# Attention and two feed-forward blocks on one core: values of the first batch on column tiles, a 16-bit sign, and a new planned order

## The chip, the cores and the metric

The program runs on one core of a Trainium2 chip. Its engines are TensorE (PE; its weight loads are listed apart as PEld), VectorE (DVE), ScalarE (ACT), GpSimd (POOL) and SyncE (SP, which here only issues DMAs). They run at the same time, each takes its own instructions in the order in which the program lists them, and semaphores tie them together. The metric is the device time of one execution in microseconds (us), lower is better.

## What is computed

```
scores = q @ k.T / 8                       # 4 batches, 8 heads, 576 x 576, head size 64
scores = where(scores >= max - tau, scores, -1e9)
x  = softmax(scores) @ v                   # 2304 x 512 when the heads stand side by side
x2 = relu(x @ w1i) ** 2 @ w1o              # 512 -> 2048 -> 512
h  = x2 @ w2i
out = (h * tanh(softplus(h))) @ w2o        # 512 -> 2048 -> 512
```

The four weight matrices come in as 64-bit floats (the kernel reads each as two 32-bit integers and builds a 32-bit float from them). Results are wanted at about the precision of 32-bit floats, so that most products are made from a high and a low part of each operand, in three matmuls instead of one.

## The kernel before

**Stages.** Tokens are cut into 9 blocks of 256. The first feed-forward block (9 token blocks, 8 slices `j` of 256 columns of the hidden layer each) can start a token block when attention has written it to DRAM; its results go to DRAM, and the second feed-forward block runs over the 9 token blocks at the end. Attention runs pair by pair (two heads side by side, 4 pairs in each of 4 batches); in a pair come units of 128 query rows (`unit`, line 703): scores on PE, a running minimum with the scaling on DVE (line 740), the exponential on ACT (line 760), the threshold with the sum on DVE (line 770), then the product with `v`.

**Two forms of attention.** Pairs of the first batch are of kind "d": their scores and values are plain 32-bit matmuls (`job_direct`, `values_direct`), and the probabilities are turned by PE transposes (line 837) and taken out of PSUM by ACT (line 850). For each of the two heads of a unit, five matmuls take a 128x128 piece of the turned probabilities as weights and 64 columns of `v` as the moving operand (line 865). Each 32-bit matmul stands in the trace as two records of weight load and matmul. The other three batches are of kind "s": a 16-bit high part (ACT, line 794) and low part (`low`, line 799, on DVE or POOL), turned by a DMA transpose.

**Weights.** Each of the four matrices is worked in 16 halves (`weights`, line 408): a load, the size by ACT (line 446), the three low bits by ACT (line 454), a clamp on DVE or POOL (line 449), the join of the two on DVE (line 461), the sign on DVE (line 467), then a high part (`to_hi`, line 495) and a low part (`to_lo`, line 505, on DVE or POOL). Layer 1's 32 halves are worked during the first 180 us, layer 2's from about 550 us on.

**Scales.** `pow2` (line 534) makes a power of two from a sum of squares, in three tiny DVE operations (lines 563, 565, 567), twice for each pair of kind "s".

**Order.** Nothing is reordered at run time. `Plan` collects every operation with its possible engines, an assumed duration on each and a due time; `order` places them by list scheduling, forwards and backwards, and so decides the order on each engine and which engine takes an operation with a choice. The numbers in `PAR` and `BIAS` shape due times and choices; buffers with a rotating choice of places (`rot`, `place`) bind the order as well. SP issues all loads and stores but the last two, in the planned order.

## Time and profile before

| | us |
|---|---|
| median of 3 runs | 1109.37 |
| lowest, highest | 1106.42, 1113.45 |
| the profiled execution | 1106.48 |
| its span, first to last instruction | 1104.7 |

The profile is of one execution. Busy time of an engine is the time in which at least one of its instructions ran; an instruction's duration holds its start-up and its tail, so durations of neighbours overlap a little. The granted clock is the share of TensorE's full clock (2.4 GHz) that it was given. Line numbers are those of the kernel before.

### The profile page before, as it was taken

The numbers are of one execution on the slowest core, as the hardware profiler recorded it, in microseconds if no ns is written. First come the engines' busy times: TensorE is split into PE (matmuls) and PEld (weight loads), VectorE is DVE, ScalarE is ACT, GpSimd is POOL, SyncE is SP. The second block draws the span as 40 slices with busy tenths as digits, with TensorE's granted clock in tenths as the row PEclk, the third lists the DMA queues.
The fourth block names the chain that finished last, engine by engine and source line by source line (L and its number), as shares of the span: only waits on it lengthen the run. The fifth ranks groups of instructions, "written<-read, shape, count | busy, mean of one in ns | idle before, by whom it ended". The sixth has DMA issues, their size and how long they took to land.

```text
span 1104.7 us, 23743 instructions
## 1 busy us (share of the span) xinstructions
PE 1071.2 (97%) x9348; PEld 967.4 (88%) x9348; DVE 743.5 (67%) x1725; ACT 775.2 (70%) x1277; POOL 84.0 (8%) x81
## 2 busy tenths in 40 slices
PE   6999989999999999999999999999999999999998
PEld 4887778888888888988999999988999889989896
DVE  4998899998797997589766149874444445443352
ACT  5788598786776876577576369977766667675584
POOL 1345021100010100010000001000000000000000
PEclk9996889999999999999999999999999999999999
DMA  8535385987777879479865024310100101000000
GB/s 239 155 108 162 94 194 125 150 175 161 154 165 144 162 155 180 78 125 167 158 206 173 25 66 146 114 59 20 39 20 20 32 9 39 20 20 20 1 20 20
DMA packets 246415, 113.75 MB, mean 103 GB/s; under 512 B 211104, under 2 KB 228000, under 8 KB 246304
## 3 DMA queue, kind: packets, MB, share of 16 engines
q1 hardware_dynamic: 246016, 111.71, 43.0%
q8 instruction: 73, 1.20, 0.4%
q10 hardware_dynamic: 288, 0.52, 0.1%
q14 instruction: 38, 0.31, 0.1%
HBM read 58.33 MB, written 14.16 MB: 66 GB/s over the span
## 4 chain that ended last, share of the span: by engine, by line
PE 74%; DVE 3%; DMA 3%; issue 1%; ACT 1%; POOL 0%; ACTq 0%; DVEq 0%; SPq 0%
PE acc L376 33%; PE h L376 19%; PE s L376 16%; PE small L376 6%; DMA pt<-hl 1%; DMA pt<-area 1%; DVE e L770 1%; DVE area L740 1%; DVE hl L799 0%; ACT e L760 0%; PE s L988 0%; ACT hl L794 0%; DVE nat L582 0%; DMA xdr<-xs 0%; DVE xo L1005 0%
## 5 line engine op out<-in xcount | busy, mean ns | idle before, releaser
L505 DVE TENSOR_TENSOR gl<-r,gh 128x512 fp32r<-128x512 f32 x85 | 58.9, 693 | 50.1 <-ACT gh L495 48.7
L1080 ACT ACT_TABLE_LOAD x70 | 89.8, 1283 | 1.3
L376 PE MATMUL s<-KT,area 64*128 64x64 f16 (+6 forms) x880 | 88.6, 323 | 2.0 <-DVE hl L740 1.3
L740 DVE TENSOR_SCALAR_CACHE_REDUCE area<-s,c 128x576 f32<-128x576 f32 x97 | 77.4, 813 | 13.2 <-PE s L376 12.7
L760 ACT ACTIVATE e<-area,m 128x576 f32<-128x576 f32 x97 | 73.0, 767 | 14.5 <-DVE area L799 6.3
L770 DVE SCALAR_TENSOR_TENSOR e<-area,n,e 128x576 f32<-128x576 f32 x97 | 78.2, 815 | 7.2 <-ACT e L760 6.4
L1033 ACT ACTIVATE r<-h 128x512 f32<-128x512 f32 x72 | 42.9, 596 | 56.1 <-PE h L376 47.2
L495 ACT ACTIVATE gh<-r 128x512 fp32r<-128x512 f32 x90 | 56.5, 627 | 36.1 <-PE acc L376 34.1
L376 PE MATMUL small<-V,pt 128*128 128x64 f16 (+1 forms) x1680 | 64.0, 194 | 7.1 <-ACT xt L891 2.7
L376 PEld LDWEIGHTS <-pt 128*128 128x128 f16 (+1 forms) x1680 | 55.2, 101 | 14.9 <-issue 6.9
L1131 DVE TENSOR_SCALAR area<-area 128x512 f32<-128x512 f32 x37 | 15.8, 426 | 77.5 <-ACT area L1084 77.3
L799 DVE TENSOR_TENSOR hl<-e,hl 128x512 f16<-128x512 f32 (+1 forms) x132 | 63.4, 491 | 4.5 <-ACT hl L794 4.3
L794 ACT ACTIVATE hl<-e 128x576 f16<-128x576 f32 x75 | 50.6, 678 | 17.9 <-DVE e L770 9.3
L505 DVE TENSOR_TENSOR gl<-e,gh 128x512 fp32r<-128x512 f32 x36 | 24.8, 690 | 39.8 <-ACT gh L495 39.6
L1084 ACT ACTIVATE area<-area 128x512 f32<-128x512 f32 x74 | 46.5, 632 | 0.5
L1084 ACT ACTIVATE area<-s 128x512 f32<-128x512 f32 x24 | 14.4, 599 | 45.7 <-PE s L376 45.6
L495 ACT ACTIVATE gh<-e 128x512 fp32r<-128x512 f32 x36 | 22.6, 629 | 33.1 <-PE acc L376 32.8
L1039 ACT ACTIVATE r<-r 128x512 f32<-128x512 f32 x72 | 45.1, 626 | 1.0
L376 PEld LDWEIGHTS <-area 64*128 64x128 f16 (+1 forms) x720 | 23.8, 97 | 22.0 <-issue 2.2
L1156 DVE TENSOR_TENSOR r<-s,area 128x512 f32<-128x512 f32 x23 | 15.9, 692 | 27.2 <-ACT area L1084 27.2
L454 ACT ACTIVATE area<-area 128x512 int32<-128x512 uint32 x46 | 31.2, 677 | 0.0
L376 PEld LDWEIGHTS s<-KT,area 64*128 64x128 f32 (+1 forms) x160 | 20.0, 201 | 12.5 <-issue 9.2
(751 smaller groups left out, 4090.3 us busy)
## 6 DMA issues: line engine op xcount, KB each, us to landing
area<-in_moe_w_in_dram SPq DMA_DIRECT2D x26, 512.0 KB, 4.4
area<-in_moe_w_out_dram SPq DMA_DIRECT2D x20, 512.0 KB, 3.5
xl<-xdr SPq DMA_DIRECT2D x36, 128.0 KB, 2.6
x2dr<-stg SPq DMA_DIRECT2D x18, 256.0 KB, 2.6
xdr<-xs SPq DMA_DIRECT2D x32, 128.0 KB, 2.2
f<-in_v_dram SPq DMA_DIRECT2D x12, 256.0 KB, 2.9
f<-in_k_dram SPq DMA_DIRECT2D x22, 128.0 KB, 2.9
area<-in_q_dram SPq DMA_DIRECT2D x20, 128.0 KB, 3.2
```

What stands on the lines that cost most here:

```text
L376: nc.tensor.matmul(o, l, r, start=start, stop=stop, skip_group_check=True)
L495: nc.scalar.activation(out=o, in_=i, func=AF.Copy)
L505: VEC[e].tensor_tensor(out=part(lo), in0=src(), in1=f32(part(hi)), op=ALU.subtract)
L740: nc.vector.tensor_scalar(out=sc(), in0=s()[:, 0:576], scalar1=c()[:, 3:4], scalar2=None, op0=ALU.mult, op1=ALU.min, accum_out=m()[:, i:i ...
L760: lambda e: nc.scalar.activation(out=ex(), in_=sc(), func=AF.Exp, bias=m()[:, i:i + 1], scale=-1.0),
L770: nc.vector.scalar_tensor_tensor(out=ex(), in0=sc(), scalar=nt()[:, i:i + 1], in1=ex(), op0=ALU.is_le, op1=ALU.mult, accum_out=l()[:, 0, u ...
L794: nc.scalar.activation(out=hl()[:, 0:576], in_=ex(), func=AF.Copy)
L799: VEC[e].tensor_tensor(out=hl()[:, a:a + n], in0=ex()[:, z:z + n], in1=hl()[:, z:z + n], op=ALU.subtract)
L1033: nc.scalar.activation(out=r(), in_=ph(), func=AF.Relu)
L1039: nc.scalar.activation(out=r(), in_=r(), func=AF.Square)
L1080: nc.scalar.preload_act_table_set({"ln": "natural_log_exp_and_others", "sig": "sigmoid_and_others"}[table])
L1084: nc.scalar.activation(out=out, in_=in_, func=func, **kw)
```

## The change

Three edits of the program, and a new set of planning numbers.

1. **Values of the first batch.** For the four full units of a group the roles are swapped: 64 columns of `v` are the weights, 128 columns of the turned probabilities move, and the two heads write to partitions 0 to 63 and 64 to 127 of one PSUM tile, alternating. So one piece of work on PE per unit instead of two; then ACT or DVE takes the tile out of PSUM, and PE turns it back by one transpose. The last, half-sized unit of a pair stays as it was.
2. **Sign.** The sign bit is written into the word of the low bits by a 16-bit operation before the join, which carries it along. For the 16 halves of the first matrix (`sp=(2, 0)`) the sign is a factor instead: ACT makes plus or minus one (`AF.Sign`), DVE or POOL multiplies.
3. **Scales.** `pow2` takes two tiny operations.

```
+MIN = (2 ** 23) * 18
 PAR = dict(
-    ex=(2, 4, 5, 2, 16, 0, 8, 6, 22, 15),
-    blk=[22.091, 76.699, 164.506, 257.524, 365.392, 394.571, 523.534, 549.17, 661.064],
-    sp=(0, 0),
+    ex=(2, 6, 5, 2, 14, 6, 15, 10, 15, 28),
+    blk=[27.468, 90.417, 206.877, 253.139, 358.304, 447.476, 540.395, 662.355, 695.332],
+    sp=(2, 0),
...
+    tv=1.3,
-    BIAS = {"V": -0.002, "A": -2.918, "P": 0.244, "S": -0.554}
+    BIAS = {"V": 2.606, "A": -6.695, "P": 2.335, "S": -0.195}
...
-            def sign(e, bits=bits, upper=upper):
-                nc.vector.scalar_tensor_tensor(
-                    out=bits(), in0=upper(), scalar=-0x80000000, in1=bits(), op0=ALU.bitwise_and, op1=ALU.bitwise_or
+            def sign(e, raw=raw):
+                z = raw().bitcast(mybir.dt.uint16)
+                nc.vector.tensor_scalar(
+                    out=z[:, :, 1], in0=z[:, :, 3], scalar1=0x8000, scalar2=None, op0=ALU.bitwise_and
...
+            mine = 2 * kind + half >= PAR["sp"][layer]
+            if mine:
+                op({"V": 0.52}, sign, x=[raw], due=due - 2.5 + O_CV, two=True)
             op({"V": 0.6}, shift, r=[raw], x=[w], due=due - 2 + O_CV, two=True)
-            if 2 * kind + half < PAR["sp"][layer]:
+            if not mine:
                 op({"A": 0.56}, factor, x=[raw], due=due - 1.9 + O_CV)
                 op({"P": 1.24, "V": 0.6}, times, r=[raw], x=[w], due=due - 1.8 + O_CV, two=True)
-            else:
-                op({"V": 0.6}, sign, r=[raw], x=[w], due=due - 1.9 + O_CV, two=True)
...
-        op({"V": 0.07}, lambda e: ts(out=isc(), in0=t()[:, 0:n], scalar1=2.0 ** -90, scalar2=None, op0=ALU.max),
+        op({"V": 0.07}, lambda e: ts(out=bits(), in0=t()[:, 0:n].bitcast(I32), scalar1=0x7F000000, scalar2=1,
+                                     op0=ALU.bitwise_and, op1=ALU.logical_shift_right),
...
+    def turned(p, j, due):
+        V, o, pts = p.V, p.o, p.pts
+        p.pts = []
+        ot = pbuf("o2", None)
+        def values(e):
+            for i in range(5):
+                d = slice(0, 128) if i < 4 else slice(64, 128)
+                for h in range(2):
+                    mm(ot()[64 * h:64 * h + 64, :], V()[d, 5 * h + i, :], pts[h]()[d, i, :], i == 0, i == 4)
+        op({"T": PAR["tv"]}, values, r=[*pts, V], w=[ot], due=due)
+        xt = sbuf(rot("pt0", "pt1"), [128, 128], F32)
+...
+        op({"A": 0.2, "V": 0.22}, evac, r=[ot], w=[xt], due=due + 0.5)
+        op({"T": 0.14}, lambda e: nc.tensor.transpose(o()[:, 128 * j:128 * j + 128], xt(), ident), r=[xt, K], w=[o], due=due + 1)
```

**What the new plan does to the order.** On PE, in the first pair, the values of a unit stood between transposes and scores like this before (`small` is the PSUM bank of the values, `V` the values, `wi5l` and `wo4h` the places that hold turned probabilities, `s` scores, `h` and `acc` turned probabilities in PSUM, `e` exponentials):

```order
L837 MATMUL acc<-ident,e_179 128x128 x5
L376 MATMUL small<-V_112,wi5l 128x64 x5
L376 MATMUL s_234<-KT_103,area 128x512
L376 MATMUL s_236<-KT_103,area 128x512
L376 MATMUL s_234<-KT_103,area 128x64
L376 MATMUL s_236<-KT_103,area 128x64
L376 MATMUL small<-V_112,wo4h 128x64 x5
L837 MATMUL h<-ident,e_232 128x128 x4
```

and now, at the same place, beginning with the last two of the ten matmuls that alternate between the two heads (`wo4l` and `wi4h` hold their turned probabilities):

```order
L380 MATMUL small<-wo4l,V_102 64x128
L380 MATMUL small<-wi4h,V_102 64x128
L380 MATMUL s_244<-KT_105,area 128x512
L380 MATMUL s_246<-KT_105,area 128x512
L380 MATMUL s_244<-KT_105,area 128x64
L380 MATMUL s_246<-KT_105,area 128x64
L910 MATMUL small<-ident,pt_253 128x128
L847 MATMUL h<-ident,e_241 128x128 x4
L847 MATMUL small<-ident,e_241 128x128
L847 MATMUL acc<-ident,e_250 128x128 x5
```

Ten matmuls of 64 output columns became ten of 128 moving columns in one piece, with the next scores and then the transpose of the result behind it.

On POOL, the first pieces of work after the constants were these before (`stg`, `wo7h` and `wo7l` are weights in the making, `wi0l` and the like finished low parts):

```order
L449 TENSOR_SCALAR wo7l<-wo7l 128x512
L449 TENSOR_SCALAR stg_270<-stg_270 128x512
L505 TENSOR_TENSOR wi0l<-stg_151,wi0h 128x512
L449 TENSOR_SCALAR stg_384<-stg_384 128x512
L505 TENSOR_TENSOR wo0l<-wo7h,wo0h 128x512
L505 TENSOR_TENSOR wo0l<-wo7l,wo0h 128x512
L449 TENSOR_SCALAR wo7h<-wo7h 128x512
```

and these now (line 481 is the factor of the sign, line 511 the low part):

```order
L453 TENSOR_SCALAR wo7h<-wo7h 128x512
L453 TENSOR_SCALAR wo7l<-wo7l 128x512
L481 TENSOR_TENSOR stg_145<-stg_145,area 128x512
L481 TENSOR_TENSOR stg_187<-stg_187,area 128x512
L511 TENSOR_TENSOR wi0l<-stg_145,wi0h 128x512
L511 TENSOR_TENSOR wi0l<-stg_187,wi0h 128x512
L511 TENSOR_TENSOR wo0l<-wo7h,wo0h 128x512
```

More of the weights' chain runs on POOL. Over the whole program POOL has 197 such pieces where it had 74, most of the new ones low parts of probabilities (line 799, 7 to 35 wide ones and 29 to 88 narrow ones); DVE has 146 instructions fewer, ACT 32 more.

## Rows read from the trace of the kernel before

**Rows 1.** Part 1 of the page: busy us, share of the span, instructions.
```profile
PE 1071.2 (97%) x9348; PEld 967.4 (88%) x9348; DVE 743.5 (67%) x1725; ACT 775.2 (70%) x1277; POOL 84.0 (8%) x81
```
**Rows 2.** Busy time by stretch: length, each engine's busy us (x instructions), granted clock, DMA.
```profile
20.00:205.00 185.00, 173.38 (x1410) 146.78 (x1409) 171.72 (x421) 147.90 (x270) 53.09 (x39) 0.92 0.57 145
205.00:552.00 347.00, 340.11 (x4090) 305.63 (x4089) 290.73 (x826) 244.76 (x417) 25.65 (x33) 1.00 0.78 153
84.00:92.00 8.00, 6.83 (x53) 5.82 (x50) 8.00 (x24) 7.32 (x15) 5.25 (x4) 1.00 0.36 115
92.00:116.00 24.00, 22.65 (x99) 18.99 (x100) 18.43 (x36) 14.74 (x30) 10.66 (x7) 0.50 0.60 162
140.00:147.00 7.00, 4.45 (x18) 3.78 (x19) 7.00 (x17) 6.63 (x13) 0.93 (x1) 0.51 0.64 146
205.00:280.00 75.00, 72.25 (x889) 64.53 (x888) 68.86 (x204) 55.69 (x96) 5.65 (x5) 1.00 0.85 167
280.00:345.00 65.00, 63.29 (x769) 56.56 (x768) 54.57 (x160) 48.23 (x84) 5.29 (x6) 1.00 0.77 162
552.00:1104.70 552.70, 547.26 (x3818) 508.59 (x3816) 274.99 (x462) 373.69 (x577) 4.43 (x2) 1.00 0.16 54
```
**Rows 3.** PE in order of time, one head's values: start, us, engine, line, tiles.
```profile
68.05 1.47 PE L376 MATMUL small<-V,wo4h 128*128 128x64 f32 x10
69.45 0.33 PE L837 MATMUL h<-ident,e 128*128 128x128 f32 x1
```
**Rows 4.** The same view, the half-sized last unit of a pair.
```profile
73.12 1.80 PE L376 MATMUL small<-V,wo4h 128*64 128x64 f32 x20
74.85 0.55 PE L837 MATMUL h<-ident,e 128*128 128x128 f32 x3
```
**Rows 5.** The same view, five transposes of 128 moving columns.
```profile
60.44 0.77 PE L837 MATMUL acc<-ident,e 128*128 128x128 f32 x5
61.07 0.66 PE L837 MATMUL h<-ident,e 128*128 128x128 f32 x4
```
**Rows 6.** PE groups by shape, first 150 us: count, busy us, mean ns, idle before.
```profile
L376 PE MATMUL s<-KT,area 64*128 64x512 f32 x64 | 24.4, 758 | 0.7 <-ACT area L681 0.7
L376 PE MATMUL s<-KT,area 64*64 64x512 f32 x16 | 4.3, 615 | 0.0
```
**Rows 7.** DVE groups by shape; the first four in 20 to 205 or 0 to 260.
```profile
L770 DVE SCALAR_TENSOR_TENSOR e<-wi4l,n,e 128x576 f32<-128x576 f32 x14 | 12.7, 908 | 2.1 <-ACT e L760 2.1
L461 DVE SCALAR_TENSOR_TENSOR stg<-stg,area 128x512 int32<-128x512 int32 x11 | 9.3, 847 | 0.0
L799 DVE TENSOR_TENSOR hl<-e,hl 128x512 f16<-128x512 f32 x23 | 15.7, 686 | 1.1 <-ACT hl L794 0.9
L799 DVE TENSOR_TENSOR hl<-e,hl 128x64 f16<-128x64 f32 x19 | 4.5, 238 | 0.0
L770 DVE SCALAR_TENSOR_TENSOR e<-area,n,e 128x576 f32<-128x576 f32 x97 | 78.2, 815 | 7.2 <-ACT e L760 6.4
L467 DVE SCALAR_TENSOR_TENSOR stg<-area,stg 128x512 int32<-128x512 int32 x13 | 8.8, 680 | 0.0
L505 DVE TENSOR_TENSOR gl<-r,gh 128x512 fp32r<-128x512 f32 x85 | 58.9, 693 | 50.1 <-ACT gh L495 48.7
L1131 DVE TENSOR_SCALAR area<-area 128x512 f32<-128x512 f32 x37 | 15.8, 426 | 77.5 <-ACT area L1084 77.3
L567 DVE TENSOR_SCALAR iscv<-iscv 128x1 f32<-128x1 f32 x12 | 1.8, 147 | 0.1
```
**Rows 8.** DVE and POOL in order of time, one overlap of the two.
```profile
91.54 1.86 DVE L770 SCALAR_TENSOR_TENSOR e<-wi4l,n,e 128x576 f32<-128x576 f32 x1
91.52 1.26 POOL L505 TENSOR_TENSOR wi3l<-stg,wi3h 128x512 fp32r<-128x512 f32 x1
```
**Rows 9.** ACT: a wide weight operation, and the small copy out of PSUM (ns min/median/max).
```profile
L454 ACT ACTIVATE area<-area 128x512 int32<-128x512 uint32 x46 | 31.2, 677 | 0.0
L850 ACT ACTIVATE wi5l<-small x18: 266/271/303, 19.1 to 129.4; 128x128 f32<-128x128 f32 x18
```
**Rows 10.** DVE in order of time: the two steps that make the second token block's operand.
```profile
206.62 0.69 DVE L1005 TENSOR_TENSOR xo<-s,xh 128x512 fp32r<-128x512 f32 x1
210.84 0.68 DVE L1005 TENSOR_TENSOR xo<-s,xh 128x512 fp32r<-128x512 f32 x1
```

More of the change, by code (lines that the diff above doesn't have):

```diff
@@ L348, in pbuf @@
     def pbuf(place, shape):
+        if place == "o2":
+            return plan.buf(place, lambda: small[:, 384:512])
         if place[0] == "o":
             z = 256 * int(place[1])
-            return plan.buf(place, lambda: small[:, z:z + 256])
+            return plan.buf(place, lambda: small[:, z:z + 256], over=("o2",) if shape == [128, 256] else ())
         return plan.buf(place, lambda: psum.tile(shape, F32, name=place, tag=place))
@@ L743, in top @@
                 )
[L745 removed]
+            op({"V": 0.74}, top, r=[s, *cr], w=[sc, m], due=due + 1 + 0.1 * i - URG)
         def most(e):
@@ L755, in unit, with whole_o @@
             head(p, g, h, u, ex, due + i * 0.5)
+    def whole_o(z):
+        return pbuf(z, [128, 256] if z == "o1" else None)
     def weigh(p, hh, j, i, sc, m, nt, due):
         ex = sbuf(place("e", "e0", "e1"), [128, 576], F32)
-        op({"A": 0.76},
+        op({"A": 0.67},
            lambda e: nc.scalar.activation(
@@ L765, in weigh @@
             p.l = sbuf(rot("l0", "l1", "l2"), [128, 3, 4], F32)
-            p.o = pbuf("o0" if p.kind == "d" else rot("o0", "o1"), None)
+            p.o = pbuf("o0", None) if p.kind == "d" else whole_o(rot("o0", "o1"))
+            p.pts = []
         l = p.l
@@ L857, in values_direct @@
             op({"A": 0.48, "V": 0.63}, lambda e: evac(e, 0), r=ts[:1], w=[pt], due=due + 3 + O_DIR)
-            op({"A": 0.3, "V": 0.3}, lambda e: evac(e, 1), r=ts[1:], w=[pt], due=due + 3 + O_DIR)
+            op({"A": 0.17, "V": 0.22}, lambda e: evac(e, 1), r=ts[1:], w=[pt], due=due + 3 + O_DIR)
+        if hh < 2:
+            p.pts.append(pt)
+            if hh == 1:
+                turned(p, u % 2, due + 7 + O_VA)
+                if last:
+                    normal(p, g, hh, due)
+            return
         def values(e):
-            for h in ((hh,) if hh < 2 else (0, 1)):
-                sl = slice(0, 128) if hh < 2 else slice(64 * h, 64 * h + 64)
+            for h in (0, 1):
+                sl = slice(64 * h, 64 * h + 64)
                 for i in range(5):
@@ L865, in values, with evac @@
                     mm(o()[sl, 64 * u:64 * u + 64], pt()[d, i, sl], V()[d, 5 * h + i, :], i == 0, i == 4)
-        op({"T": 1.3}, values, r=[pt, V], w=[o], due=due + 7 + O_VA)
-        if last:
-            normal(p, g, hh, due)
+        op({"T": 1.6}, values, r=[pt, V], w=[o], due=due + 7 + O_VA)
+        normal(p, g, hh, due)
+    def turned(p, j, due):
+        V, o, pts = p.V, p.o, p.pts
+        p.pts = []
+        ot = pbuf("o2", None)
[6 more added lines that the diff above has]
+        xt = sbuf(rot("pt0", "pt1"), [128, 128], F32)
+        def evac(e):
+            if e == "A":
+                nc.scalar.activation(out=xt(), in_=ot(), func=AF.Copy)
+            else:
+                nc.vector.tensor_copy(out=xt(), in_=ot())
+        op({"A": 0.2, "V": 0.22}, evac, r=[ot], w=[xt], due=due + 0.5)
+        op({"T": 0.14}, lambda e: nc.tensor.transpose(o()[:, 128 * j:128 * j + 128], xt(), ident), r=[xt, K], w=[o], due=due + 1)
     def normal(p, g, hh, due):
@@ L877, in norm @@
             def norm(e):
+                src = o().rearrange("p (j h d) -> p h j d" if p.kind == "d" else "p (h j d) -> p h j d", h=2, j=2)
                 nc.vector.tensor_tensor(
                     out=xs().rearrange("p j (h d) -> p h j d", h=2),
-                    in0=o().rearrange("p (h j d) -> p h j d", h=2, j=2),
+                    in0=src,
                     in1=l()[:, 2, :].rearrange("p (h j) -> p h j", h=2).to_broadcast([128, 2, 2, 64]),
```

31 lines of the change are left out of this document (14 added, 17 removed).

## The prediction

> **What bounds the kernel now.** I read first the page's busy times: PE runs for 1071.2 of 1104.7 us, DVE and ACT for about 70% each, POOL for 8% [rows 1]. A busy PE need not be a PE at its peak, so the second view was busy time by stretch [rows 2]. From 552 us on PE idles 5.4 us of 552.7, and all of it but a fraction is the store at the very end: that stretch is matmuls of the feed-forward blocks, and nothing that this edit touches shortens it. From 205 to 552 PE idles 347 - 340.1 = 6.9 us while DVE is busy 84% of the time. The stretch from 20 to 205 is another matter: PE 173.4, DVE 171.7 and ACT 147.9 of 185 us. There the first batch's attention, the making of layer 1's weights and the start of the first feed-forward block lie on each other, and PE and DVE are both at 93%. Also there the granted clock falls to 0.50, the lower level of 1.2 GHz, from 92 to 116 us and again from 140 to 147; before the first fall PE had been busy only 6.8 of 8 us, and DVE 8.0 of 8. While the clock was low PE was busy 22.65 us, which is work of about 11.3 us at full clock, so the first fall cost at most 11 us.
>
> So the end time is PE's whole work plus PE's idle time plus what the low clock takes, and nearly all the idle time lies before 205 us. An edit gains if it takes work from PE, or idle time from PE's early stage, and loses if it makes DVE, ACT or POOL later there.
>
> **Values on column tiles.** Before, one head's values take 69.45 - 68.05 = 1.40 us from start to start [rows 3], two heads 2.80 us; four pairs with four full units each make 16 such units, 44.8 us at full clock. Now a unit is ten 32-bit matmuls with 128 moving columns, two records each. A record of 128 moving columns in 32 bits takes (61.07 - 60.44) / 5 = 0.126 us [rows 5]. If the two heads, on the two halves of the array's columns, run side by side, that is ten steps, 1.26 us; if they run one after the other, 20 steps, 2.52 us. The last piece of each head has only 64 rows; for entering and leaving it I add 0.2 us, an estimate from the half-sized unit, where 20 records with 64 columns take 74.85 - 73.12 = 1.73 us [rows 4], 0.087 each, with two such pieces in it. The transpose of the result adds 0.126. So 1.59 or 2.85 us against 2.80: a gain of 16 x 1.21 = 19.4 us, or a loss of 0.8.
>
> Which one? No row here shows two column halves alone at work. The nearest are scores: one record of 512 columns by itself would take 4 x 0.126 = 0.50 us, yet row halves that alternate between heads take 24.4 / 64 = 0.38 each and quarters (half the rows, half the columns) 4.3 / 16 = 0.27 [rows 6]. So halves of the array do run beside each other, and I take 19.4 us. The Trainium skill says so in general (TensorEngine Tiling (Array Packing), Key Properties: tiles load weights and multiply independently), and by it the gain is the 19.4; but the same section has the array drain when the tiling changes, and the new piece enters column tiles, quarter tiles and full transposes anew in each unit. By a drain as long as the 0.2 us for each of the three changes the gain would be 16 x 0.81 = 13 us; rows 4 contain such changes and leave room for about that.
>
> The copy out of PSUM is new: all 16 went to ACT in the planned order, 0.27 us each by the nearest row [rows 9], 4.3 us. PE doesn't wait for it where the next scores stand in between, as they do in the first pair; a wait not covered would cost at most 0.27 + 0.126, 6 us for all 16.
>
> **Sign and factor.** Before 205 us all 32 halves of layer 1 are worked. Their sign cost 32 x 0.68 = 21.8 us of DVE [rows 7]. Now 16 halves have the 16-bit operation; the trace has none of its kind. Between a one-input operation on dense numbers, 0.426, and the two-input one that it replaces, 0.68, I take 0.60, nearer the latter, since its words lie 8 bytes apart: 9.6 us. Of the 16 products DVE has 7 (0.69 each, 4.8 us) and POOL 9. DVE gains 7.4 us (5 to 10 by the bounds). ACT gets 16 x 0.68 = 10.8 us [rows 9]. Layer 2's 32 halves gain 32 x 0.08 on a DVE that is half idle there: nothing. The scales save one operation of 0.15 us [rows 7], 24 in all and some five before 205: 0.7 us.
>
> **POOL for DVE.** By the planned order POOL has 63 pieces before the second token block where it had 39. DVE is rid of six wide low parts (0.69), seven narrow ones (0.24) and six low parts of weights and hidden values (0.69), and gets four clamps (0.43): 4.1 + 1.7 + 4.1 - 1.7 = 8.2 us. With sign and scales DVE is 16.3 us lighter. Against it: POOL and DVE slow each other. Beside POOL's work the threshold ran at 0.908 where its usual mean is 0.815, the join at 0.847 against 0.68 for its twin [rows 7]: 14 x 0.093 + 11 x 0.167 = 3.1 us in two groups that fill 22 of DVE's 172 busy us. Other lines are held up less often; three times the 3.1 for all of DVE, over 39 POOL pieces, is about 0.25 us each. For 24 more: 6 us. DVE's net relief up to 205 us is then 10.3 us.
>
> **The sum.** In the early stage PE is 19.4 us lighter, DVE 10.3, and ACT 15.1 heavier (147.9 + 15 = 163 of what would be 175). Since PE and DVE were equally loaded, the later of the two sets the end: 10 us earlier, what PE has over turns into idle time. The second token block's operand, made by DVE from 206.62 to 211.5 [rows 10], should come about 10 us earlier. The planned order has then done 12 fewer matmuls of the feed-forward block, 12 x 0.12 = 1.4 us, which remain to be done. After that POOL takes another 22 wide and 52 narrow low parts and 11 others from DVE: 15.2 + 12.5 + 7.6 = 35 us, less 0.25 for each of 87 additional pieces, 22 us. DVE gains 13 us in a stretch where PE idled 6.9; I count half of that, 3.5, and 2 more for idle time that the early stage now avoids because the first token block stands earlier in the order. Together 10.3 - 1.4 + 3.5 + 2 = 14.4 us from the profiled 1106.48: 1092. The median of the runs lies 2.9 above the profiled one, so I forecast **1094**. (About 1% is what a measurement of this kernel can tell from no change.)
>
> **Rivals.**
>
> *Everything counts.* If DVE keeps up (0.426 for the sign, POOL for nothing: 19.5 + 6 us) the 19.4 of PE arrive in full, and the low clock may not come: 1106.5 - 19.4 + 1.4 - 5.5 = 1083, with half of the 11 us back 1077; median 1080. For it: DVE's idle 13 us before 205 show that it isn't always last. Against it: ACT gets fuller.
>
> *Column halves one after the other.* PE keeps its 44.8 us; only DVE's relief is left, of which PE, as loaded as before, takes little: 1106.5 - 3 + 0.8, median about 1107. Against it: rows 6.
>
> *ACT or the low clock.* ACT at 93% is then the third full engine, and PE, with less to do, sits idle more often in just the stage in which the clock fell after 1.2 us of idle in 8. Another low stretch like that from 92 to 116 takes up to 11 us: 1094 + 11 = 1105.
>
> *Slower: POOL locks DVE out.* Once, at 91.54, the threshold took 1.86 us beside a POOL piece of 1.26 [rows 8], 1.04 over its mean. If every additional POOL piece did this, up to 205 us DVE loses 24 x 1.04 = 25 us and gains 16.3: 9 us later. From 205 to 345 the order has 35 more pieces, 36 us, against 12 us of work taken from DVE; DVE's slack there is 140 - 123.4 = 16.6 us [rows 2], so another 8 us. 1106.5 + 17, median about 1126. It decides from 16.3 / 24 = 0.68 us per piece; the rows speak for 0.25. By the Trainium skill (SBUF — State Buffer, "SBUF: two separate sides") POOL and a DVE operation with two inputs take the second port by an exclusive lock for a whole instruction; by that rule the 1.04 would be usual. The trace has it only now and then: most of DVE's instructions beside POOL are not lengthened, since POOL waits as often as DVE does.
>
> **How the numbers follow.** Forecast 0.55 (its own range 1086 to 1102, from 2.4 us on either side for the sign, 6 for the changes of tiling, 4 for POOL); everything counts 0.12; one after the other 0.12; ACT or clock 0.10; POOL locks 0.11. Faster than 1098.3: 0.46 of the forecast's 0.55, 0.11 of the first rival, 0.01 of the others: 0.58. Slower than 1120.5: the last rival and a little: 0.12. The rest, 0.30, within 1%. Leaving out one in ten on either side the range goes from 1079 to 1114.
>
> **What would show it.** A unit's values of 1.3 to 1.6 us on PE right; 2.5 or more, the halves run in turn. The 16-bit sign near 0.60; the threshold (the two-input line) at a mean under 0.88 in the early stage, else POOL costs more than taken. The second block's operand near 196 us, and PE's idle time from 20 to 205 grown by a few us while its busy time falls. The forecast is wrong if that operand comes after 205, or if the low clock covers much more than 31 us.

## The result, and the profile after

The changed kernel takes 1119.3 us (median of 12 runs, 1114.4 to 1124.3) where the kernel before took 1106.3 beside it: a ratio of 1.0118, 95% interval 1.0095 to 1.0140. It is slower by about 13 us. The forecast was 1094, range 1079 to 1114.

Part 1 of the page of after, to be read against [rows 1]:

```profile
PE 1064.2 (95%) x9364; PEld 950.0 (85%) x9364; DVE 734.2 (66%) x1579; ACT 787.5 (70%) x1309; POOL 205.5 (18%) x204
```

and its busy time by stretch, with the columns of [rows 2] (length, busy us of PE, PEld, DVE, ACT and POOL, granted clock, DMA):

```profile
20.00:205.00 185.00, 160.11 (x1404) 124.08 (x1401) 174.72 (x394) 158.50 (x301) 80.82 (x62) 0.90 0.57 148
205.00:552.00 347.00, 333.73 (x3965) 298.82 (x3964) 273.54 (x710) 242.51 (x413) 99.71 (x120) 0.98 0.78 146
552.00:1119.00 567.00, 559.42 (x3964) 520.56 (x3963) 281.30 (x463) 378.61 (x585) 24.11 (x15) 1.00 0.18 56
```

Up to 205 us PE is busy 13.3 us less than before, and DVE, which should have been lighter, 3 us more. PE's idle time there went from 11.6 to 24.9 us, and from 205 to 552 from 6.9 to 13.3. The low clock comes more often. This is the same view for all the stretches at 0.50 but the one at the very end:

```profile
76.10:79.50 3.40, 3.24 (x12) 2.30 (x12) 3.30 (x12) 2.58 (x5) 3.08 (x3) 0.50 0.59 182
96.60:117.10 20.50, 18.76 (x87) 12.87 (x87) 17.34 (x40) 16.37 (x33) 5.38 (x4) 0.50 0.60 155
134.10:140.90 6.80, 6.52 (x42) 5.07 (x43) 6.48 (x16) 4.73 (x11) 0.00 (x0) 0.50 0.66 153
168.30:171.70 3.40, 3.24 (x15) 3.24 (x16) 3.40 (x7) 3.40 (x7) 1.62 (x1) 0.50 1.26 169
185.30:188.70 3.40, 3.40 (x19) 3.40 (x18) 3.15 (x8) 3.03 (x5) 2.53 (x2) 0.50 0.92 97
294.60:301.40 6.80, 6.21 (x49) 6.05 (x50) 3.66 (x8) 2.23 (x3) 0.81 (x1) 0.50 0.82 193
458.40:465.20 6.80, 6.22 (x44) 5.12 (x45) 5.15 (x14) 2.91 (x4) 2.20 (x3) 0.50 0.38 78
sum 51.10, PE 47.59 PEld 38.05 DVE 42.48 ACT 35.24 POOL 15.61; mean PE 6.80 PEld 5.44 DVE 6.07 ACT 5.03 POOL 2.23
```

With these rows a span splits into three parts: PE's work at full clock, what the low clock takes (half of PE's busy time in those stretches), and PE's idle time.

| | span | work at full clock | lost to the clock | idle |
|---|---|---|---|---|
| before | 1104.7 | 1071.2 - 13.5 = 1057.7 | (22.65 + 4.45) / 2 = 13.5 | 33.5 |
| after | 1119.0 | 1064.2 - 23.8 = 1040.4 | 47.59 / 2 = 23.8 | 54.8 |
| difference | +14.3 | -17.3 | +10.3 | +21.3 |

So the edit did take 17.3 us of work from PE, and more than all of it came back as idle time and low clock. The steps that release PE didn't move forward. DVE makes the second token block's operand here at (start, us, line; the answer to [rows 10]):

```profile
208.12 0.68 DVE L1047 TENSOR_TENSOR xo<-s,xh 128x512 fp32r<-128x512 f32 x1
213.32 0.68 DVE L1047 TENSOR_TENSOR xo<-s,xh 128x512 fp32r<-128x512 f32 x1
```

which is 1.5 us later than before and not 10 earlier. The operand of the seventh block, the first that holds rows of the last batch, comes at 564.65 us where it came at 553.03 (the first row is after's, the second before's):

```profile
564.65 0.69 DVE L1047 TENSOR_TENSOR xo<-s,xh 128x512 fp32r<-128x512 f32 x1 [2.11 <-ACT KT L450]
```
```profile
553.03 0.69 DVE L1005 TENSOR_TENSOR xo<-s,xh 128x512 fp32r<-128x512 f32 x1 [2.01 <-ACT xh L1000]
```

From there to the end PE is as good as full in both, 554.3 us in after and 551.7 in before. The seventh operand is the step to watch: it takes in all that happened ahead of it. (These starts are those of the one profiled execution of each kernel; that of no_sign, below, is 3.1 us under its median and that of after_ahead 3.7 under.)

### The profile page after: what moved, and what is told of

Its sections match the earlier page's. It is cut to its first block, busy times and chain, and to the rows that moved or that the text cites. A ratio compares the mean times of both kernels' runs of the same rounds, so it can differ in the third digit from the quotient of the medians.

```text
span 1119.0 us, 23855 instructions
## 1 busy us (share of the span) xinstructions
PE 1064.2 (95%) x9364; PEld 950.0 (85%) x9364; DVE 734.2 (66%) x1579; ACT 787.5 (70%) x1309; POOL 205.5 (18%) x204
## 4 chain that ended last, share of the span: by engine, by line
PE 66%; DVE 6%; ACT 4%; DMA 4%; issue 3%; SPq 2%; POOL 0%; DVEq 0%; ACTq 0%
PE acc L380 29%; PE h L380 16%; PE s L380 14%; PE small L380 6%; DMA pt<-hl 2%; DVE e L780 1%; DVE area L472 1%; DMA pt<-area 1%; DVE area L746 1%; SPq L377 1%; DMA area<-in_moe_w_out_dram 1%; DVE hl L809 0%; ACT area L458 0%; DVE nat L588 0%; ACT hl L804 0%
## 5 line engine op out<-in xcount | busy, mean ns | idle before, releaser
L380 PE MATMUL s<-KT,area 64*128 64x64 f16 (+6 forms) x880 | 91.2, 333 | 7.9 <-DVE area L746 3.2
L809 POOL TENSOR_TENSOR hl<-e,hl 128x64 f16<-128x64 f32 (+1 forms) x84 | 65.5, 794 | 161.3 <-ACT hl L804 139.2
L769 ACT ACTIVATE e<-area,m 128x576 f32<-128x576 f32 x100 | 76.1, 770 | 23.0 <-POOL hl L809 6.8
L780 DVE SCALAR_TENSOR_TENSOR e<-area,n,e 128x576 f32<-128x576 f32 x100 | 82.9, 841 | 10.1 <-ACT e L769 8.4
L511 DVE TENSOR_TENSOR gl<-r,gh 128x512 fp32r<-128x512 f32 x71 | 50.7, 714 | 54.1 <-ACT gh L501 52.7
L380 PEld LDWEIGHTS <-pt 128*128 128x128 f16 (+1 forms) x1680 | 55.5, 102 | 19.6 <-DMA pt<-hl 6.7
L809 DVE TENSOR_TENSOR hl<-e,hl 128x512 f16<-128x512 f32 (+1 forms) x64 | 43.5, 682 | 10.1 <-ACT hl L804 9.9
L380 PEld LDWEIGHTS <-area 64*128 64x128 f16 (+1 forms) x720 | 23.8, 98 | 25.9 <-issue 6.5
L809 POOL TENSOR_TENSOR area<-e,area 128x64 f16<-128x64 f32 (+1 forms) x39 | 29.4, 767 | 74.4 <-ACT area L804 74.3
L511 POOL TENSOR_TENSOR gl<-r,gh 128x512 fp32r<-128x512 f32 x19 | 26.6, 1398 | 55.4 <-ACT gh L501 55.4
```

The source lines that it names most:

```text
L380: nc.tensor.matmul(o, l, r, start=start, stop=stop, skip_group_check=True)
L511: VEC[e].tensor_tensor(out=part(lo), in0=src(), in1=f32(part(hi)), op=ALU.subtract)
L769: lambda e: nc.scalar.activation(out=ex(), in_=sc(), func=AF.Exp, bias=m()[:, i:i + 1], scale=-1.0),
L780: nc.vector.scalar_tensor_tensor(out=ex(), in0=sc(), scalar=nt()[:, i:i + 1], in1=ex(), op0=ALU.is_le, op1=ALU.mult, accum_out=l()[:, 0, u ...
L809: VEC[e].tensor_tensor(out=hl()[:, a:a + n], in0=ex()[:, z:z + n], in1=hl()[:, z:z + n], op=ALU.subtract)
```

## The experiments

**Edits and numbers apart.** The change has three edits and a new table of numbers, from which the planner makes a new order on every engine. Two kernels take one half each.

edits_old_numbers: after, with before's table (`tv` added).

```diff
-    cd=(-62.495, -4.588, 25.036),
-    ex=(2, 6, 5, 2, 14, 6, 15, 10, 15, 28),
+    cd=(-145.092, 2.133, 28.758),
+    ex=(2, 4, 5, 2, 16, 0, 8, 6, 22, 15),
...
-    BIAS = {"V": 2.606, "A": -6.695, "P": 2.335, "S": -0.195}
+    BIAS = {"V": -0.002, "A": -2.918, "P": 0.244, "S": -0.554}
```

> The three edits with the numbers of before (due times, biases of the engines, lent places), so POOL gets about 17 more pieces and not 123, and no half of layer 1 goes by the factor on ACT. Theory 1 (the additional POOL pieces lengthen DVE's instructions and eat what PE saved): without them PE's 16 shorter value units count in part, the clock falls less often, 1095 to 1103 us, and the threshold's mean before 205 us stays near 0.82. Theory 2 (PE's saving turns into idle time and low clock whatever POOL does, because DVE sets the early stage): 1106 to 1112. Theory 3 (the 16-bit sign, 0.80 instead of 0.68 us, on all 32 halves of layer 1 here): 4 us more on DVE before 205 us, 1108 to 1112.

Measured: 1122.2 us, 1.0143 of before (1.0108 to 1.0178).

numbers_only: before, with after's table.

```diff
-    BIAS = {"V": -0.002, "A": -2.918, "P": 0.244, "S": -0.554}
+    BIAS = {"V": 2.606, "A": -6.695, "P": 2.335, "S": -0.195}
...
```

> The kernel before with the numbers of after alone: about 105 more POOL pieces, half of the halves of input weights by the factor on ACT, none of the edits. Theory 1 (POOL pieces lengthen DVE, and what they give back arrives late): 1120 to 1130 us, DVE's sums before 205 us not lower than before, and the jumps near 160 to 185, 290 and 460 us that after shows. Theory 2 (it is the lighter PE that idles and loses the clock): PE is as heavy as before, 1104 to 1110.

Measured: 1124.6 us, 1.0180 (1.0124 to 1.0235).

Either half alone is slower than before; the intervals of the two and of after overlap, so their own order is open. No theory had edits_old_numbers at 1122: POOL has hardly more to do there than before (43 pieces up to 205 us for 39), so POOL's share can't be the only cause. Its second operand came at 199.2 us, 7 earlier than before, and its seventh at 561.0, 8 later. The values' gain was there at 200 us and lost behind it. In numbers_only the second operand came at 220.7 us, 14 later than before. Its time is in theory 1's range, but DVE, busy 157.3 us from 20 to 205 where before has 171.7, is not what fills that stage there, so theory 1's reason isn't shown by it.

**The sign.** sign32: after, in its own order, the sign by a two-input operation on 32 bits.

```diff
-                nc.vector.tensor_scalar(
-                    out=z[:, :, 1], in0=z[:, :, 3], scalar1=0x8000, scalar2=None, op0=ALU.bitwise_and
+                nc.vector.scalar_tensor_tensor(
+                    out=lower(), in0=upper(), scalar=-0x80000000, in1=lower(), op0=ALU.bitwise_and, op1=ALU.bitwise_or
                 )
```

> The changed kernel in its own order on every engine, its 16-bit sign replaced by one 32-bit two-input operation that does the same (and, or) in the same place. If the 16-bit operation is dear in itself (0.80 against 0.68): 16 x 0.12 = 2 us less DVE before 205 us, time 1116 to 1119. If its price doesn't reach the end: 1119 within 2 us. If the two-input form is held up more beside POOL's pieces: 1119 to 1123.

Measured: 1120.1 us, 1.0133 (1.0098 to 1.0169). The sixteen signs took 12.4 us instead of 13.2, 0.05 less each, and that doesn't reach the end.

no_sign: the same order, the sign of layer 1 on one column.

```diff
-                    out=z[:, :, 1], in0=z[:, :, 3], scalar1=0x8000, scalar2=None, op0=ALU.bitwise_and
+                    out=z[:, 0:N_, 1], in0=z[:, 0:N_, 3], scalar1=0x8000, scalar2=None, op0=ALU.bitwise_and
```

> The changed kernel in its own order; the sign of layer 1's 16 halves is written for one column of 512 only, so 16 x 0.74 = 12 us of DVE's work before 205 us are gone (the signs of these weights are left out). Theory B (DVE sets the early stage): the second block's operand 8 to 12 us earlier and the end 1108 to 1112. Theory A (PE's order and later waits): the operand earlier by less than 4 us, the end 1116 to 1120.

Measured: 1116.1 us, 1.0065 (1.0039 to 1.0091), with the second operand at 203.71 and the seventh at 557.71. Sixteen signs of 0.82 us became 0.14 each, 11 us less for DVE; the operand came 4.4 earlier and the end about 6. So DVE is on the path of the early stage, but not alone: the operand lies between the two expectations, and so does the time when it is taken by its ratio (1.0065 x 1106.3 = 1113.5 us).

**POOL's pieces.** low_on_dve: after, in its own order on every queue, and each piece that POOL had is issued on DVE in its place.

```diff
             o = plan.ops[n]
-            o.fn(o.eng)
+            o.fn("V" if o.eng == "P" and "V" in o.opts else o.eng)
```

> The changed kernel in its own order, but what POOL had (low parts, clamps, products) issued on DVE at the same place; POOL is left with nothing but its set-up. DVE then has 197 more pieces to do, 63 of them before the second token block's operand, and nothing beside it on POOL. If a POOL piece costs DVE about 0.6 us in lengthened instructions, as DVE's sums suggest, the pieces themselves (0.24 to 0.69) cost about as much as they did beside it: 1112 to 1122, the threshold's mean back at 0.74 to 0.80. If a POOL piece costs DVE 0.25, as forecast, DVE gets some 15 to 20 us more before 205 us and the time is 1130 or more.

Measured: 1114.5 us, 1.0079 (1.0037 to 1.0122); second operand 201.94, seventh 558.40. DVE does the 197 pieces that POOL had and the kernel is not slower but 4 us faster (the two intervals overlap; a second pair stands below). From 20 to 205 us DVE is busy 181.4 us for 174.7: most of the time of the pieces comes back. Where from shows in DVE's groups from 20 to 205 us (count, busy us, mean ns, idle before). In after:

```profile
L780 DVE SCALAR_TENSOR_TENSOR e<-hl,n,e 128x576 f32<-128x576 f32 x29 | 26.1, 904 | 1.3 <-ACT e L769 1.1
L780 DVE SCALAR_TENSOR_TENSOR e<-wi4l,n,e 128x576 f32<-128x576 f32 x13 | 12.5, 959 | 1.7 <-ACT e L769 1.6
L755 DVE TENSOR_SCALAR n<-m,tt 128x2 f32<-128x2 f32 x22 | 10.1, 460 | 0.0
L465 DVE SCALAR_TENSOR_TENSOR stg<-stg,area 128x512 int32<-128x512 int32 x8 | 6.9, 858 | 0.0
L809 DVE TENSOR_TENSOR hl<-e,hl 128x512 f16<-128x512 f32 x6 | 6.1, 1021 | 0.0
L453 DVE TENSOR_SCALAR stg<-stg 128x512 f32<-128x512 f32 x12 | 6.3, 528 | 0.0
L472 DVE TENSOR_SCALAR area<-area 128x512 uint16<-128x512 uint16 x6 | 5.7, 958 | 0.0
```

and in low_on_dve, where nothing runs on POOL:

```profile
L780 DVE SCALAR_TENSOR_TENSOR e<-hl,n,e 128x576 f32<-128x576 f32 x29 | 23.6, 820 | 0.1
L780 DVE SCALAR_TENSOR_TENSOR e<-wi4l,n,e 128x576 f32<-128x576 f32 x13 | 10.7, 820 | 0.2
L809 DVE TENSOR_TENSOR hl<-e,hl 128x512 f16<-128x512 f32 x13 | 8.9, 693 | 0.2 <-ACT hl L804 0.2
L453 DVE TENSOR_SCALAR stg<-stg 128x512 f32<-128x512 f32 x17 | 7.3, 430 | 0.3 <-ACT stg L450 0.3
L465 DVE SCALAR_TENSOR_TENSOR stg<-stg,area 128x512 int32<-128x512 int32 x8 | 5.6, 696 | 0.0
L755 DVE TENSOR_SCALAR n<-m,tt 128x2 f32<-128x2 f32 x23 | 5.2, 228 | 0.0
L472 DVE TENSOR_SCALAR area<-area 128x512 uint16<-128x512 uint16 x6 | 4.6, 765 | 0.0
```

The threshold costs 0.904 and 0.959 us beside POOL and 0.820 without it, the join (L465) 0.858 and 0.696, the wide low part 1.021 and 0.693. The small step on two columns (L755) doubles on the mean, 0.460 for 0.228: 22 x 0.23 = 5 us in operations that I had not costed at all. It isn't slowed evenly: five of the 22 took 1.23 to 1.25 us, the 14 that lay beside no POOL piece 0.22 to 0.23. Taking from each DVE instruction of the first 205 us the median of the same operation and shape in low_on_dve, and adding up, before comes to 10.2 us over 39 POOL pieces and after to 25.2 over 62. The mean before is 0.26 us per piece, close to the 0.25 that I took; the 23 additional pieces cost 15.0 / 23 = 0.65 each. Nearly all of it is a few long hold-ups: ten DVE instructions beside POOL lost over 0.5 us in before, 9.6 us together, and 25 in after, 24.3 together, about 1 us each. Others beside POOL ran at their usual time (135 lay beside a POOL piece in before, 177 in after). That an engine waited for a result of POOL is not the reason: from 20 to 205 us the profile puts no wait of after down to POOL.

**The values, in either order.** old_values_new_order: after's order, the values in the old form at the place of the turned ones, without copy and transpose. (It serves for its time alone, since its results are of no use; the matmuls are as many as before.)

```diff
-                    mm(ot()[64 * h:64 * h + 64, :], V()[d, 5 * h + i, :], pts[h]()[d, i, :], i == 0, i == 4)
+                    c = 128 * j + 64 * h
+                    mm(o()[:, c:c + 64], pts[h]()[d, i, :], V()[d, 5 * h + i, :], i == 0, i == 4)
```

> The changed kernel in its own order with the values in the old form: both heads' 40 matmul records at the place of the turned ones, each straight into its columns of the output; no copy, no transpose. PE gets back 16 x 1.27 = 20 us before 130 us. Theory A (PE's work counts): 1132 to 1138 us. Theory B (DVE is what PE waits for there): most of it falls into idle time that PE has now (24.9 us from 20 to 205), 1119 to 1126.

Measured: 1131.0 us, 1.0186 (1.0156 to 1.0216). In this order the turned values are worth (1.0186 - 1.0118) x 1107 = 7.5 us of the 20 that they take from PE. That lies between the theories again. (The sixteen copies on ACT go with them; the second operand is 12.5 us later than in after.)

turned_same_order: before's order on DVE, POOL and SP, both heads turned at the place of the later one's values; copies and transposes put in behind.

```diff
+        pending.append((now[0] + GO[0], lambda: nc.scalar.activation(out=xt, in_=ot, func=AF.Copy)))
+        pending.append((now[0] + GO[1], lambda: nc.tensor.transpose(o()[:, 128 * j:128 * j + 128], xt, ident)))
...
+    now, done, held, GO = [0.0], set(), [], (1.5, 2.3)
```

> The kernel before in its own order on DVE, POOL and SP, with the values of the first batch turned (both heads at the place of the second one's values; 16 copies on ACT and 16 transposes some 1.5 and 2.3 us behind in the plan's time). PE is about 20 us lighter before 130 us and nothing else changes. Theory A (the saving is sound, and the new order loses it): 1088 to 1096 us. Theory B (DVE sets the early stage and attention's pace up to the later token blocks, so PE only gets ahead and waits): the second block's operand at 204 to 208 as before, PE idle in place of the saving, 1100 to 1108.

Measured: 1122.9 us, 1.0117 (1.0095 to 1.0140): neither theory. The waits from 20 to 135 us say why (engine and line that waited, for whom, us in total, times, longest):

```profile
PE small L898 <- ACT xs L897: 10.0, 8, 2.9
ACT wo4h L851 <- PE small L377: 9.2, 7, 2.5
ACT wi5l L851 <- PE small L377: 5.6, 3, 2.5
```

PE waited 10 us for the copies where I had put them. And ACT waited 14.8 us to write the next turned probabilities, since both of the two buffers for them (`pt`, in places wo4h and wi5l) are held until the second head is there; before, the first is free after its own head's values, and ACT waited 8.2 us on the values there. This variant shows what a badly placed copy costs, and says nothing on the edit itself.

turned_sign_same_order adds the 16-bit sign.

```diff
             def shift(e, raw=raw):
+                z = raw().bitcast(mybir.dt.uint16)
+                nc.vector.tensor_scalar(
+                    out=z[:, :, 1], in0=z[:, :, 3], scalar1=0x8000, scalar2=None, op0=ALU.bitwise_and
+                )
```

> The same, and all halves of layer 1 and 2 with the 16-bit sign, written first into the low word, with the shift behind it in the sign's place. Before 205 us DVE gets 32 x 0.10 = 3 us more, by the durations in after (0.80 for 0.68 us). Theory B: 2 to 4 us slower than with the values alone, since DVE sets the stage. Theory A: the same as with the values alone, within 2 us.

Measured: 1120.8 us, 1.0099 (1.0076 to 1.0122), no slower than without. As in sign32 the sign doesn't reach the end.

**Orders moved by one number.** Four kernels differ from before or after in one number of the table, by 1.0; no operation is added or dropped.

```diff
-    ahead=(17.742, 18.622, 5.391, 14.998, 19.512, 19.512, 20.853, 23.144, 34.262, 35.066),
+    ahead=(17.742, 18.622, 5.391, 14.998, 20.512, 19.512, 20.853, 23.144, 34.262, 35.066),
```

> The kernel before, with one number of its table moved by 1.0 (the fifth of AHEAD, 19.512 to 20.512, the lead of the third batch's attention over its token block); the planner gives a new order on every engine, no operation is added or taken away. Theory C (the order of before is one good draw, and any new order loses about what the variants with new orders lost): 0.8 to 2% slower, 1116 to 1128 us. Theory D (what after lost lies in its edits and in POOL's larger share): within 0.4% of before.

> The same with another number, START from -26.594 to -25.594. Theory C: 0.8 to 2% slower than before. Theory D: within 0.4%.

> The changed kernel, the fifth of AHEAD moved by 1.0 (24.058 to 25.058), so a new order on every engine. Theory C: after is itself one draw, tuned like before; nudged 0.5 to 1.5% slower than after, 1125 to 1136 us. Theory D: within 0.4% of after's 1119.

> The changed kernel, START moved by 1.0 (-23.978 to -22.978). Theory C: 0.5 to 1.5% slower than after. Theory D: within 0.4% of 1119.

Measured: before_ahead 1117.9 (1.0099, 1.0066 to 1.0132), before_start 1119.0 (1.0089, 1.0050 to 1.0128), after_ahead 1113.5 (1.0059, 1.0028 to 1.0090), after_start 1113.6 (1.0037, 1.0010 to 1.0065). Theory C held for the two orders near before's and had the sign wrong for the two near after's; theory D held for none. An order moved a little away from before's loses about 1%, with the same operations; moved away from after's it gains 0.6 to 0.8%. Before_ahead, by stretch:

```profile
20.00:205.00 185.00, 172.43 (x1407) 145.90 (x1408) 171.84 (x424) 149.26 (x272) 44.41 (x35) 0.93 0.59 143
205.00:552.00 347.00, 333.50 (x3958) 298.00 (x3957) 283.69 (x801) 242.29 (x411) 32.92 (x42) 0.99 0.80 147
```

Up to 205 us it is before over again (its second operand comes at 207.18, before's at 206.62); then PE idles 13.5 us where before idled 6.9, just what after does in that stretch, and the seventh operand comes at 564.93, as in after. So the 10 us that after loses between 205 and 565 us can come from the order alone, with none of the edits. (The two don't lose them at the same place: before_ahead is behind by the fourth operand, after not until later.) The orders near after's show the same from the other side. They keep the edits and POOL's share, and need hardly more than before between the two operands (start of each, us):

| | second | seventh | between |
|---|---|---|---|
| before | 206.62 | 553.03 | 346.4 |
| before_ahead | 207.18 | 564.93 | 357.8 |
| before_start | 208.11 | 567.14 | 359.0 |
| numbers_only | 220.71 | 567.77 | 347.1 |
| edits_old_numbers | 199.25 | 561.01 | 361.8 |
| after | 208.12 | 564.65 | 356.5 |
| after_ahead | 204.78 | 554.01 | 349.2 |
| after_start | 206.14 | 554.86 | 348.7 |
| low_on_dve | 201.94 | 558.40 | 356.5 |

By the medians of these neighbours, orders that nobody picked, the changed kernel is the faster one, 1113.5 against 1118 or 1119. With two orders on either side, and intervals that overlap, this is a hint and no more.

**The clock.** after_filled: after's order, with matmuls that no one needs in ten of PE's waits; before_filled: the same in six of before's.

```diff
+    FILL = {277: 8, 291: 12, 296: 4, 373: 7, 375: 7, 553: 4, 1275: 6, 1378: 12, 1320: 6, 2031: 10}
...
+            for _ in range(FILL.get(n, 0)):
+                to = o.fn.aim()
+                if to.shape[1] == 128:
+                    nc.tensor.transpose(to, ident, ident)
+                else:
+                    mm(to, ident, ident[:, 0:64], True, True)
             o.fn(o.eng)
```

> The changed kernel in its own order; in front of ten of PE's waits (93.1, 95.2, 102.4, 127.5, 130.5, 131.9, 284.6, 289.3, 293.6 and 455.6 us in the trace of after) 76 matmuls on the identity are put, about as long as the wait, into the PSUM columns that the waiting instruction then overwrites. PE gets some 11 us of work that no one needs. If it is the clock that cost after its time (23.8 us lost in 53 us of low clock, where before lost 13.5): the falls at 96.6, 134, 294.6 and 458 don't come, PE's loss goes down by 10 us, time 1106 to 1113. If the low clock covers only idle time: 1119 to 1126.

> The kernel before with 39 such matmuls ahead of six waits of PE (87.5, 91.3, 102.5, 137.1, 139.8 and 141.0 us in its trace). If the clock's two falls (92.2 and 140.0, 13.5 us lost) follow from these waits and count at the end: 1096 to 1103 us. If DVE sets the stage and PE would wait anyhow: 1106 to 1112.

Measured: after_filled 1116.7 (1.0074, 1.0042 to 1.0106), before_filled 1110.5 (1.0017, 0.9981 to 1.0054). All the low stretches of after_filled but the one at the end:

```profile
101.60:105.00 3.40, 3.40 (x25) 2.41 (x24) 2.29 (x5) 3.40 (x8) 0.00 (x0) 0.50 0.94 328
108.40:115.20 6.80, 5.89 (x20) 4.39 (x22) 6.80 (x20) 5.14 (x10) 1.30 (x1) 0.50 0.21 46
142.60:146.00 3.40, 2.94 (x13) 2.94 (x14) 3.40 (x4) 3.40 (x7) 3.40 (x4) 0.50 0.01 2
183.50:186.90 3.40, 3.40 (x22) 2.79 (x18) 3.40 (x9) 2.91 (x6) 1.33 (x3) 0.51 0.76 177
sum 17.00, PE 15.63 PEld 12.53 DVE 15.89 ACT 14.85 POOL 6.03; mean PE 3.91 PEld 3.13 DVE 3.97 ACT 3.71 POOL 1.51
```

The falls at 294.6 and 458.4 us are gone and the low clock around 100 us is halved; PE loses 15.63 / 2 = 7.8 us to the clock and not 23.8. And yet the second operand moved only from 208.12 to 207.63, the seventh from 564.65 to 562.26, and the end by 2.6 us (4.9 by the ratios). The page of after_filled says where the 16 us went:

```profile
PE 1063.0 (95%) x9462; PEld 950.4 (85%) x9462; DVE 733.6 (66%) x1579; ACT 786.9 (70%) x1309; POOL 203.5 (18%) x204
```

In its span of 1116.8 us PE's work at full clock is 1063.0 - 7.8 = 1055.2 us, 14.8 more than in after, and its idle time 53.8 for 54.8. So the added matmuls took nearly all that the clock gave back. They were meant to lie in PE's waits, but the idle time did not shrink by them: either PE waited elsewhere instead, or they outlasted the waits that they were put into. The run doesn't tell these apart, and so doesn't show what the low clock costs at the end. Before_filled doesn't either, since in its profiled execution the clock was still low for 27 us, where before has 31. The twelve executions of after go along with their clock: the two with a mean of 0.985 have spans of 1112.6 and 1112.9 us, the six at 0.978 or less 1115.5 to 1122.6. Whether the low clock made them longer, or the same waits made both, these numbers don't say.

**POOL left out, once more, and with orders of its own.** after_ahead_low is low_on_dve on the order of after_ahead.

```diff
-            o.fn(o.eng)
+            o.fn("V" if o.eng == "P" and "V" in o.opts else o.eng)
```

> The changed kernel with the moved number of after_ahead (1113.5 us), and what POOL had issued on DVE at the same place of its order. If POOL's pieces cost DVE more than their own work, as in the first order (1119.3 to 1114.5): 4 to 6 us less, 1107 to 1110. If that gain was an accident of one order: 1111 to 1118.

Measured: 1110.5 us, 1.0028 (0.9998 to 1.0059), 3 to 4 us below after_ahead. So a second order agrees in sign and size by the medians, though these two intervals overlap as well. The profiled executions don't show it: that of after_ahead is its fastest of ten, and the second operand comes at 204.78 us with POOL and at 204.72 without.

The last three have the turned values, the two-operation scales and the 32-bit sign, and tables of numbers found by a search over plans. In replanned_no_pool the planner can't give low parts and clamps to POOL; in replanned_pool_dear it counts more of the overlap against DVE; replanned has the costs of after.

```diff
-            op({"V": 0.34, "P": 1.45}, clamp, x=[w], due=due - 3 + O_CV, two=True)
+            op({"V": 0.34}, clamp, x=[w], due=due - 3 + O_CV, two=True)
...
-        op({"V": 0.6, "P": 1.24}, fn, r=[src, hi], w=[lo], due=due, two=True)
+        op({"V": 0.6}, fn, r=[src, hi], w=[lo], due=due, two=True)
```

> The turned values and the two-operation scales kept, the sign by the 32-bit two-input operation; the table of numbers searched again for the shortest plan under the planner's own costs (its plan is 3.9 us shorter than after's), with 199 POOL pieces. If an order is only as good as its costs, and POOL's price in them is too low: no better than the moved tables of after, 1110 to 1118 us.

> The same edits, but in the planner's costs a POOL piece holds DVE up for all of the overlap, not for 0.6 of it, and DVE a POOL piece for 0.3 and not 0.15; the numbers searched again under these costs. The search leaves POOL with none of the low parts, clamps or products. Its plan is 1.3 us shorter than after's. Theory (POOL's pieces cost DVE more than they save, and the plan should know it): 1104 to 1111 us, below after_ahead_low's 1110.5 if the search does any good. If POOL's pieces were worth having: 1113 to 1120.

> The same edits and costs as replanned, with POOL taken from the choice for low parts and clamps; numbers searched again, plan 0.5 us shorter than after's. The same theory: 1104 to 1111; the other: 1113 to 1120.

Measured: replanned 1112.6 (1.0043, 1.0016 to 1.0070), replanned_pool_dear 1102.1 (0.9946, 0.9920 to 0.9972), replanned_no_pool 1101.4 (0.9931, 0.9904 to 0.9959). The two without POOL beat both kernels; the one with 199 POOL pieces, whose plan the planner took for the shortest of the three, is 1% behind them. Each of the three has an order of its own, and in the orders above one moved number alone was worth up to 1%, so this 1% can't be put down to POOL; that rests on the two pairs with one order each. The page of replanned_no_pool and its first stretch:

```profile
PE 1053.5 (96%) x9364; PEld 941.3 (86%) x9364; DVE 751.1 (68%) x1775; ACT 782.5 (71%) x1295; POOL 0.8 (0%) x7
20.00:205.00 185.00, 165.57 (x1492) 128.47 (x1493) 175.81 (x466) 151.22 (x286) 0.00 (x0) 0.92 0.60 147
```

and its second and seventh operand:

```profile
199.52 0.69 DVE L1046 TENSOR_TENSOR xo<-s,xh 128x512 fp32r<-128x512 f32 x1
545.06 0.69 DVE L1046 TENSOR_TENSOR xo<-s,xh 128x512 fp32r<-128x512 f32 x1 [0.15 <-ACT xh L1041]
```

DVE issues 466 instructions up to 205 us where after has 394, in 175.8 us where after needs 174.7. The second operand is 8.6 us earlier than in after, the seventh 19.6. Not run is the kernel before with a table searched without POOL; what part of the 0.7% the turned values have, and what part POOL's absence by itself, is therefore open.

## Why the prediction was wrong

**Values on column tiles: right.** One unit of after on PE (start, us, line, tiles; the two heads alternate):

```profile
41.65 0.32 PE L380 MATMUL small<-wo4l,V 128*64 128x128 f32 x1
41.66 0.32 PE L380 MATMUL small<-wi4h,V 128*64 128x128 f32 x1
...
43.04 0.66 PE L847 MATMUL h<-ident,e 128*128 128x128 f32 x4
```

The heads start 10 ns apart and the unit takes 43.04 - 41.65 = 1.39 us, of the 1.46 that I gave it without the transpose. By the split above the work that left PE is 17.3 us, for 19.4. The rival of column halves in turn falls. For the copies (L905) the transposes waited 3.1 us in 5 waits up to 205 us, inside the bound of 6.

**The sign: mis-sized, outside its bounds.** I took 0.60 us between 0.426 and 0.68. It takes 0.765 us where POOL is silent (the L472 row of low_on_dve), so it is dearer than the two-input operation that it replaced. In after 14 of the 16 took 0.71 to 0.78 us, and two, held up beside POOL, 1.07 and 1.73. Up to 205 us the 16 signs cost 13.2 us, 0.82 each, so sign and factor relieve DVE by 21.8 - 13.2 - 4.8 = 3.8 us and not by 7.4. But sign32 shows that this term alone moves the end by less than can be measured.

**POOL for DVE: the step that failed.** I charged 0.25 us for each additional piece, a mean over the pieces of before, and so let DVE win 10.3 us up to 205. The additional ones cost 0.65, and DVE's busy time from 20 to 205 us went up from 171.72 to 174.72. With no relief on DVE my own sum gives nothing for the early stage but PE's idle time: PE and DVE were equally loaded, PE alone got lighter, and "the later of the two sets the end". The threshold, which should have stayed under 0.88 us on the mean, takes 0.904 and 0.959 in its two large groups, and the operand comes at 208 us, not at 196. The rival with POOL had the right mechanism: it put the deciding price at 0.68 us per piece, and the runs showed about that. By its 1.04 for every piece it would have been 1126. I gave it 0.11 because most instructions beside POOL looked undisturbed. They are so in after too; what grew is the number of those that are held up, from 10 to 25, each for about the 1.04 us that I had seen once. A mean per piece hid that. The rule of the Trainium skill that I weighed there (SBUF — State Buffer, "SBUF: two separate sides", the exclusive lock of the second port for a whole instruction) fits hold-ups of this kind, as long for an instruction of 0.22 us (1.0 us more) as for one of 0.82 (up to 1.1 more). In numbers_only 55 pieces made 15 of them, so their number isn't the pieces' alone.

How much of the miss this makes is known only in part. Low_on_dve, the same order without POOL, gets back 6.2 of the 11.8 us that the second operand is late against my sum, and about 4 at the end. For the other 5.6 the new table is a rival that no run rules out: in numbers_only it alone puts that operand 14 us later, with DVE idle for 28 of 185 us.

**From 205 us on: a term with the wrong sign.** I added 3.5 us for DVE's relief and 2 for idle time avoided. From second to seventh operand before needs 553.0 - 206.6 = 346.4 us and after 564.65 - 208.12 = 356.5. I had read in [rows 2] that DVE is busy 84% there and PE nearly full, and took a lighter DVE for a gain. DVE did get lighter, 273.5 us busy for 290.7, and its instructions were lengthened by only about 14 us over 121 POOL pieces from 205 to 565, less than the 0.25 each that I charged; it was worth nothing. In after PE's work between the two operands is 2.3 us less than in before, the low clock takes 6.2 more and idle time 6.3 more. Low_on_dve needs the same 356.5 us, so in this order POOL's pieces are not the reason. The order is, by the table of starts above: before_ahead, with before's operations and almost before's table, needs 357.8, and after_ahead and after_start, with all edits and POOL's share, 349.2 and 348.7. Before's 346.4 is nothing rare, since numbers_only has 347.1 and replanned_no_pool 345.5; some orders keep that pace and some lose some 10 us, and I had no term for which. Which chain it is that sets the pace from 205 to 565 us (DVE, ACT, the DMA transposes or their queue) these runs don't settle.

**The low clock: more than foreseen.** It covers 51 us and not 31, as I named for a sign of a wrong forecast, and PE loses 10.3 us more to it than before, about what the rival "ACT or the low clock" put on another low stretch. Its other half failed: ACT is busy 158.5 of 185 us and not full. What the 10.3 us cost at the end stays open, as said with after_filled.

Against the profiled 1120.8 us the sum of 1092 was wrong by 28.7: 11.8 at the second operand (208.1 for 196.3), 15.6 from there to the seventh (356.5 for 340.9), 1.3 behind it (554.3 for 553.1). So the larger part is the stretch in which the order decides. (The 22, 52 and 11 pieces of the sum are 85, not the 87 charged; that is half a microsecond.)

## What to carry to other kernels

A mean price read off the kernel before isn't the price of the next piece: where the change gives a helper engine more to do beside a full one, reckon the new pieces also at the dearest overlap that the trace shows (here 0.25 was the mean, 1.04 the dearest, and 0.65 came), and add the small instructions, which lose most by share. Follow the step that sets the last full stretch free (here the seventh operand), not only the first one that the edit touches. And where a table of numbers makes the order, the order is part of the change: move one number of either kernel by a little, and see how far the time goes, before giving the difference to the edits.

## What the runs showed of the hardware

- A single-input operation on 16-bit words 8 bytes apart (128x512) took 0.765 us on DVE in a kernel without POOL's pieces, the two-input one on 32-bit words that it replaced 0.68 in before [rows 7].
- Two heads on the two halves of the array's columns, in 32 bits, start 10 ns apart and keep a step of about 0.11 us together.
- A DVE operation on 128x2 elements took 0.228 us in low_on_dve, without POOL. In after five of 22 took 1.23 to 1.25 us beside a POOL piece, and the 14 beside none 0.22 to 0.23. Over all DVE instructions up to 205 us, 25 lost over 0.5 us beside POOL, 24.3 us together.
- Matmuls that no one needs, put ahead of PE's waits in after, kept the granted clock at its upper level in places where it had fallen: at 0.50 for 51 us in after, for 17 in after_filled. They took 14.8 us of PE's time themselves, and the median moved by 2.6 us.
